# Two float16 parts in place of two float32r parts in the key and gate products of a channel mix

## The chip, the cores and the metric

The kernel runs on one core of one Trainium2 chip. The metric is device time of one execution in microseconds (us), the median of several runs. Three runs of the kernel before took 794.37, 796.18 and 797.66 us.

## The reference

Attention with a forgetting bias (8 batches, 8 heads, 576 positions, head width 64), and on its output `x` (8 x 576 rows of 512) a channel mix:

```python
xk = mu_k * x + (1.0 - mu_k) * x_prev      # x_prev: x one position earlier, zero first
xr = mu_r * x + (1.0 - mu_r) * x_prev
k = np.maximum(xk @ w_k, 0.0)              # 512 x 1024
v = k * k @ w_v                            # 1024 x 512
r = 1.0 / (1.0 + np.exp(-(xr @ w_r)))      # 512 x 512
return r * v
```

The weights arrive as float64 words and the result is wanted close to float32. A product therefore is made of three matmuls of operands in two parts, a high one and what is left: high·high, low·high, high·low.

## The kernel before

**Order.** Every piece of work is a task with an engine, an estimated duration, its buffers and a due time. `Plan.run` passes over all tasks forward and backward 30 times, keeps the order with the earliest modelled end, and emits each engine's instructions in it. The order is therefore fixed when the program is built, and any changed estimate moves instructions on all engines. `or_on` (through `or_dve`, `or_act`, `or_pool`) lets the planner put one task on a second engine. On PE, `pe(..., n, m, cycle)` charges `n * cycle` ns for n streamed columns.

**Attention.** 36 visits, each two heads of a batch. Batches 0 and 1 (12 visits, "plain") turn their weights on TensorE; batches 2 to 7 (24 visits) turn them by DMA and take values and weights as two float16 parts. There `greatest` finds on VectorE the largest amount of the values of each partition, `laid_out` spreads it over all rows by a small matmul, and three short VectorE and POOL instructions make the scale (`scales`). Queries and keys are split on POOL (`split_qk`), values too (`split_v`). Each visit stores its output to `x_d` in DRAM.

**Channel mix.** 18 chunks of 256 positions; `channel_mix` follows the attention by as much as `MARGIN` says. Of each chunk:
- `mix(0)` and `mix(1)`: for each pair of 128-row blocks, ACT multiplies x of one position by mu (L1432), VectorE adds the other position times 1 - mu (`mu1`, L1448), ACT copies the high part (L1470), VectorE subtracts for the low part (L1476). Parts are float32r.
- `hidden(fp)`, 4 times: 24 matmuls of 256 columns (L1504) into one bank, ACT Relu (L1516), VectorE product to the square (L1534), and two parts `kh`, `kl` (L1539, L1543).
- `gate(tt)`, twice: 12 matmuls of 512 columns (L1556), and tanh on ACT.
- `output(tt)`, twice: 24 matmuls of 512 columns with w_v (L1581), product with the gate (L1592), store.

So a chunk has 96 matmuls of 256 columns with w_k, 24 of 512 with w_r and 48 of 512 with w_v, and all 18 have 1728, 432 and 864.

**Weights.** `load_weight` joins two 32-bit words to a float32 (`whole`) on ACT, POOL and three VectorE steps (L654, L661, L668), copies the high part (L675) and subtracts for the low one (L680, on POOL or VectorE). All 8 blocks of w_k and 4 of w_r are loaded ahead of the visits, 8 of w_v in chunk 0.

When the TensorE queue has nothing ready in the first 40 us, the planner puts in small bfloat16 matmuls of no use (L434).

Of the kernel before, what the change touches and what calls it, by code (L numbers as in the profile page):

```python
# [11 lines left out]
F32 = mybir.dt.float32  # L12
# [42 lines left out]
class Plan:  # L55
# [24 lines left out]
    def __init__(self):  # L80
        self.tasks, self.slots, self.due = [], {}, 0.0
        self.columns, self.idle, self.busy_from = {}, None, None
        self.quarters = {}
        self.issues = {}
        self.others = {}
# [51 lines left out]
    def or_on(self, i, engine, ns, emit):  # L137
        self.others[i] = engine, ns, emit
# [198 lines left out]
def forgetting_attention_then_channel_mix(  # L337
# [20 lines left out]
    P = 128  # L358
# [30 lines left out]
    def pe(emit, reads, writes, n, m=P, cycle=1.05 / 2.4, k=P):  # L389
# [120 lines left out]
    mu = fixed(const.tile([P, 2, NC], F32, name="mu"))  # L510
    mu1 = fixed(const.tile([P, 2, NC], F32, name="mu1"))
# [46 lines left out]
    def early_sums():  # L558
# [15 lines left out]
        dve(lambda: nc.vector.memset(one.get(), 1.0), [], [one], n)  # L574
# [21 lines left out]
    def load_mu():  # L596
        for i, m in enumerate((moe_mu_k, moe_mu_r)):
            dma(lambda i=i, m=m: nc.sync.dma_start(mu.ap[:, i, :], m), [], [(mu, i)], 20)
        dve(
            lambda: nc.vector.tensor_scalar(  # L600
                out=mu1.ap, in0=mu.ap, scalar1=-1.0, scalar2=1.0, op0=ALU.mult, op1=ALU.add
            ),
            [(mu, 0), (mu, 1)], [mu1], 8,
        )

    def load_weight(name, c, o, w, due, x):
# [3 lines left out]
        tag = f"w_{name}_{c}_{o}"  # L610
        words = sbuf([P, 512, 2], tag, 1, I32)
        block = weight[name, c, o] = sbuf([P, 2, 512], tag, 1, F32R)
        hi, lo = (block, 0), (block, 1)
        plan.due = due - WAHEAD
# [9 lines left out]
        plan.due = due  # L624

        if name == "k":
            ps = bank(1, *(("xp", 1) if x % 3 == 2 else ("m", 2)))
        else:
            ps = bank(1, *(("xp", 1) if x % 2 == 0 else ("m", 2)))
        whole = sbuf([P, 512], (("xh1", "xl1") if name != "v" else ("x", "r"))[x % 2])  # L630

# [3 lines left out]
        def bits():  # L635
# [3 lines left out]
        last3 = sbuf([P, 512], "last3", 1, I32)  # L639
# [6 lines left out]
            [words], [last3], 512, 210, 1.0,  # L646
# [19 lines left out]
        )  # L666
        dve(
# [5 lines left out]
        )  # L673
        or_pool(
# [4 lines left out]
        def low(engine):  # L679
            engine.tensor_tensor(  # L680
                out=block.get()[:, 1], in0=whole.get(), in1=f32(block.get()[:, 0]), op=ALU.subtract
            )

        or_dve(
            pool(lambda: low(nc.gpsimd), [whole, hi], [lo], 512, 190, 2.0),
            lambda: low(nc.vector), 512, 200,
        )

# [10 lines left out]

    def greatest(n, vn):
        am = sbuf([P, 1], "am", 2, BF16)
        dve(
            lambda: nc.vector.tensor_reduce(
                out=am.get(), in_=vn.get()[:, 0:NQ].rearrange("p k h d -> p (k h d)"),
                axis=mybir.AxisListType.X, op=ALU.max, apply_absolute_value=True,
            ),
            [vn], [am], P * NQ,  # L710
# [3 lines left out]
    def laid_out(ps, a, am):  # L714
        pe(
            lambda: nc.tensor.matmul(
                ps.get()[:, a : a + P], am.get().broadcast_to([P, P]), ident16.ap,
                start=True, stop=True,
            ),
            [am, ident16], [ps], P, P, 1 / 2.4,  # L720
        )
        scales = sbuf([P, 3], "scales", 2)
# [5 lines left out]
        dve(  # L728
            lambda: nc.vector.tensor_reduce(
                out=own(0), in_=ps.get()[:, a : a + P], axis=mybir.AxisListType.X, op=ALU.max,  # L730
            ),
            [ps], [(scales, 0)], P,
        )
        dve(
            lambda: nc.vector.tensor_scalar(
                out=own(0), in0=own(0), scalar1=1.0e-28, scalar2=1.0 / HALF, op0=ALU.max, op1=ALU.mult,
            ),
            [], [(scales, 0)], 1,
        )
# [1092 lines left out]
```

## Time and profile before

| | |
|---|---|
| runs | 794.37, 796.18, 797.66 us |
| profiled execution | 794.96 us, of which the span from the first to the last instruction is 793.3 us |
| PE busy | 774.9 us, 98% |
| VectorE (DVE) busy | 625.0 us, 79% |
| ScalarE (ACT) busy | 607.8 us, 77% |
| GpSimd (POOL) busy | 414.1 us, 52% |
| granted TensorE clock | 1.00 of full speed in every stretch |

A matmul's duration in the trace is longer than the time by which it holds up the next one, since matmuls overlap. What one costs is read from a run of them back to back: the time of the run divided by their number. PEld, the loading of the stationary operand, overlaps the matmul before.

### The profile page before, as it was taken

What the parts mean: (1) busy time and instruction counts of PE and PEld (TensorE: products, weight loads), DVE (VectorE), ACT (ScalarE), POOL (GpSimd) and SP (SyncE); (2) the same over time, 40 slices, a digit from 0 to 9 for tenths busy, and PEclk for the clock granted to TensorE, in tenths of its full rate; (3) what the DMA queues carried; (4) which work ended last, traced back from release to release, by engine and by line L of the source; (5) the groups of instructions that cost most, each with busy time, mean ns of one, the idle gap of its engine ahead of it and who ended that gap; (6) DMA issues with size and microseconds to landing.
All of it is one profiled execution on the core that took longest, in us unless ns stands there. A gap on an engine that the chain in (4) does not pass through costs nothing. (4 is left out here: it accounts for less than half of the span.)

```text
span 793.3 us, 17133 instructions
## 1 busy us (share of the span) xinstructions
PE 774.9 (98%) x5369; PEld 654.2 (82%) x5369; DVE 625.0 (79%) x1886; ACT 607.8 (77%) x1847; POOL 414.1 (52%) x505
## 2 busy tenths in 40 slices
PE   9999899999999999999999999999999999999998
PEld 8878678868788887878887989787979788888996
DVE  7998978679888898779988898888889887444531
ACT  5998988779878887879888887878888887444420
POOL 5896966664756746666656565467466610000000
PEclk9999999999999999999999999999999999999999
DMA  7967364379999888977989898897978756111000
GB/s 223 287 222 236 100 178 121 86 174 191 188 189 191 175 205 171 206 134 174 214 177 189 191 188 200 157 180 179 213 140 193 144 117 118 50 54 41 14 27 26
DMA packets 220155, 124.15 MB, mean 157 GB/s; under 512 B 180192, under 2 KB 193504, under 8 KB 220064
## 3 DMA queue, kind: packets, MB, share of 16 engines
q1 hardware_dynamic: 220064, 123.06, 69.2%
q8 instruction: 42, 0.69, 0.4%
q14 instruction: 49, 0.40, 0.2%
HBM read 61.21 MB, written 19.33 MB: 102 GB/s over the span
## 5 line engine op out<-in xcount | busy, mean ns | idle before, releaser
L1504 PE MATMUL m<-xh,w_k 128*128 128x256 f32 x976 | 193.4, 286 | 2.9 <-DVE kl L1543 2.2
L1581 PE MATMUL m<-w_v,kh 128*128 128x512 f32 x528 | 177.3, 400 | 0.0
L1504 PEld LDWEIGHTS m<-xh,w_k 128*128 128x128 f32 x976 | 156.6, 189 | 8.5 <-DVE kl L1543 5.1
L1504 PE MATMUL m<-xl,w_k 128*128 128x256 f32 x488 | 138.6, 284 | 0.0
L1581 PEld LDWEIGHTS m<-w_v,kh 128*128 128x128 f32 x528 | 99.0, 189 | 19.8
L1581 PE MATMUL m<-w_v,kl 128*128 128x512 f32 x264 | 105.5, 399 | 0.2 <-DVE kl L1543 0.2
L1432 ACT ACTIVATE xp<-x,mu 128x256 f32<-128x256 f32 (+3 forms) x179 | 76.0, 425 | 27.3 <-DMA x<-x_d 15.3
L839 POOL TENSOR_TENSOR KH<-raw,KH 64x576 fp32r<-64x576 f32 x64 | 91.2, 1425 | 5.6 <-ACT KH L828 1.4
L1504 PEld LDWEIGHTS m<-xl,w_k 128*128 128x128 f32 x488 | 92.2, 189 | 1.0
L1556 PE MATMUL m<-w_r,xh 128*128 128x512 f32 x264 | 91.3, 400 | 0.5 <-DVE kl L1543 0.5
L1448 DVE SCALAR_TENSOR_TENSOR xp<-x,mu,xp 128x256 f32<-128x256 f32 (+3 forms) x184 | 76.5, 416 | 18.6 <-ACT xp L1432 15.5
L863 POOL TENSOR_TENSOR QL<-raw,G 64x576 fp32r<-64x576 f32 (+1 forms) x64 | 85.3, 1333 | 3.8 <-ACT G L852 1.0
L1019 ACT ACTIVATE s<-s,nm 128x64 f32<-128x64 f32 (+2 forms) x144 | 61.3, 425 | 17.4 <-DVE nm L1004 15.9
L859 POOL CAST G<-raw 128x576 fp32r<-128x576 f32 x48 | 32.0, 666 | 78.7 <-issue 56.1
L1050 DVE SCALAR_TENSOR_TENSOR W<-s,rinv,W 128x64 f16<-128x64 f32 (+2 forms) x144 | 64.2, 456 | 11.0 <-ACT W L1044 9.2
L1044 ACT ACTIVATE W<-s,rinv 128x64 f16<-128x64 f32 (+2 forms) x144 | 63.5, 456 | 6.2 <-DVE rinv L1035 5.1
L1050 DVE SCALAR_TENSOR_TENSOR W<-t,rinv,W 128x320 f16<-128x320 f32 (+1 forms) x96 | 61.4, 645 | 6.5 <-ACT W L1044 5.7
L1019 ACT ACTIVATE t<-t,nm 128x320 f32<-128x320 f32 (+1 forms) x96 | 55.3, 576 | 8.4 <-DVE nm L1004 5.3
L1476 DVE TENSOR_TENSOR xl<-xp,xh 128x512 fp32r<-128x512 f32 x72 | 49.4, 687 | 12.4 <-ACT xh L1470 12.0
L1004 DVE CUSTOM_DVE_ANT_0 t<-t,lower 128x512 f32<-128x512 f32 (+1 forms) x96 | 57.2, 601 | 2.4 <-PE t L992 2.0
L1556 PEld LDWEIGHTS m<-w_r,xh 128*128 128x128 f32 x264 | 49.5, 188 | 11.2 <-DVE kl L1543 1.4
L1044 ACT ACTIVATE W<-t,rinv 128x320 f16<-128x320 f32 (+1 forms) x96 | 57.5, 609 | 1.7 <-DVE rinv L1035 1.0
(206 smaller groups left out, 1990.6 us busy)
## 6 DMA issues: line engine op xcount, KB each, us to landing
raw<-in_q SPq DMA_DIRECT2D x112, 144.0 KB
raw<-in_k SPq DMA_DIRECT2D x32, 288.0 KB
vn<-in_v SPq DMA_DIRECT2D x24, 384.0 KB
out<-g SPq DMA_DIRECT2D x36, 256.0 KB
x_d<-xT SPq DMA_DIRECT2D x28, 288.5 KB
x<-x_d SPq DMA_DIRECT2D x11, 514.0 KB
w_k<-in_moe_w_k SPq DMA_DIRECT2D x8, 512.0 KB
w_v<-in_moe_w_v SPq DMA_DIRECT2D x8, 512.0 KB
```

The source lines that it names most:

```text
L839: lambda own=own, other=other, K=K: nc.gpsimd.tensor_tensor(out=K.get()[other], in0=k.get()[own], in1=f32(K.get()[own]), op=ALU.subtract),
L863: lambda x=x, QQ=QQ, QL=QL: nc.gpsimd.tensor_tensor(out=QL.get()[0:64, 0:nq], in0=x.get()[0:64], in1=f32(QQ.get()[0:64]), op=ALU.subtract,),
L1004: lambda: nc.vector.tensor_tensor_reduce(out=ps.get()[:, :n], in0=ps.get()[:, :n], in1=mask(), scale=-SCALE, scalar=3.0e38, op0=ALU.add, o ...
L1019: lambda: nc.scalar.activation(ps.get()[:, :n], ps.get()[:, :n], AF.Exp, bias=nm.get()[:, i + o : i + o + 1], scale=-1.0, accum_out=sums.g ...
L1044: lambda: nc.scalar.activation(part(0), ps.get()[:, :n], AF.Copy, scale=rinv.get()[:, i : i + 1]),
L1050: lambda: nc.vector.scalar_tensor_tensor(out=part(1), in0=ps.get()[:, :n], scalar=rinv.get()[:, i : i + 1], in1=part(0), op0=ALU.mult, op1 ...
L1432: lambda z=z: nc.scalar.activation(to(*z), source(1, *z), AF.Copy, scale=mu.ap[:, which, c + z[0] : c + z[0] + 1]),
L1448: lambda z=z: nc.vector.scalar_tensor_tensor(out=to(*z), in0=source(0, *z), scalar=mu1.ap[:, which, c + z[0] : c + z[0] + 1], in1=to(*z), ...
L1476: lambda: nc.vector.tensor_tensor(out=lo.get()[:, cc], in0=src(), in1=f32(hi.get()[:, cc]), op=ALU.subtract),
L1504: lambda u=u, f=f, c=c, n=n, w=w, x=x: nc.tensor.matmul(ps.get()[:, u * CT : (u + 1) * CT], weight["k", c, f // 4].get()[:, w, f % 4 * P : ...
L1556: lambda c=c, n=n, x=x, w=w: nc.tensor.matmul(ps.get(), x.get()[:, c, ts], weight["r", c, 0].get()[:, w], start=c == 0 and n == 0, stop=c ...
L1581: lambda f=f, n=n, x=x, w=w: nc.tensor.matmul(ps.get(), x.get()[:, f, ts], weight["v", f, 0].get()[:, w], start=f == 0 and n == 0, stop=f ...
```

## The change

Products with w_k and w_r take two float16 parts. Float16 has a short range of exponents, so both operands are scaled by powers of two:
- `load_rows` finds the largest amount of each weight row (128 x 512, both halves of w_k), cuts it to its exponent (`steps`), and multiplies the row by its inverse times 2^14 on POOL before the two parts are made.
- `scale_mu` multiplies mu and 1 - mu (now one tile `mus`) by `steps`, and finds the largest of them over all rows by a small matmul (`most`).
- `greatest` now runs for the plain visits too; the largest value of each batch is kept in `tops`. `scale_chunk` makes of `tops` and `most` a power of two for the batches of a chunk and the scaled `shares`, in five or six short VectorE instructions. It runs again only when the set of batches differs from that of the chunk before: 15 times for each of the two products.
- Relu, square and tanh take the scale out again, by constants or by a scalar of each partition.

The number of matmuls stays. The planner's numbers change as well: columns of float16 matmuls are charged less, of float32r more, `MARGIN` is 5000, a few tasks may go to another engine than before (`free` holds that to batches 0 and 1 and chunks 0 to 2), some memsets and the low part of the weights are now always on POOL, and w_r is loaded in chunk 0 after the second `hidden` and not ahead of the visits.

```diff
-    def pe(emit, reads, writes, n, m=P, cycle=1.05 / 2.4, k=P):
+    def pe(emit, reads, writes, n, m=P, cycle=1.07 / 2.4, k=P):
...
     def or_on(self, i, engine, ns, emit):
-        self.others[i] = engine, ns, emit
+        if self.free:
+            self.others[i] = engine, ns, emit
...
+    def all_rows(ps, am, a=0):
+        pe(
+            lambda: nc.tensor.matmul(
+                ps.get()[:, a : a + P], am.get().broadcast_to([P, P]), ident16.ap,
+                start=True, stop=True,
...
+    def scale_mu(which):
+        both = mus.ap[:, which]
+        am = sbuf([P, 1], "am", 2, BF16)
+        ps = bank(1, "xp", 1)
...
+                out=both, in0=both, in1=steps.ap[:, which].unsqueeze(1).broadcast_to([P, 2, NC]),
...
+            [(steps, (which, c)) for c in range(NC)], [(mus, which)], 8,
...
+        all_rows(ps, am)
...
+                out=most.ap[:, which : which + 1], in_=ps.get()[:, 0:P],
...
+    def load_rows(which, c, due, step):
...
+            block = weight[name, c, o] = sbuf([P, 2, 512], f"w_{name}_{c}_{o}", 1, F16)
...
+            join(words[o], ps, whole, (found, o, lambda o=o: found.get()[:, o : o + 1]))
...
+                own().bitcast(I32), own().bitcast(I32), EXPONENT, op=ALU.bitwise_and
...
+            lambda: nc.vector.reciprocal(found.get()[:, 2:3], own()), [key], [(found, 2)], 1,
...
+                lambda whole=whole: nc.gpsimd.tensor_scalar(
+                    out=whole.get(), in0=whole.get(), scalar1=found.get()[:, 2:3], scalar2=2.0**14,
...
+            parts_of(block, whole)
+        if c == NC - 1:
+            scale_mu(which)
...
+    def scale_chunk(which, groups):
...
+                out=own(0), in_=tops.ap[:, a:e].rearrange("p a b -> p (a b)"),
...
+                out=own(1), in0=own(0), scalar1=most.ap[:, which : which + 1], scalar2=1.0e-30,
...
+                own(1).bitcast(I32), own(1).bitcast(I32), EXPONENT, op=ALU.bitwise_and
...
+        dve(lambda: nc.vector.reciprocal(own(2), own(1)), [], [scaled], 2)
...
+                out=shares.get(), in0=mus.ap[:, which], scalar1=own(2), scalar2=0.25,
...
         def mix(which):
-            hi = sbuf([P, NC, CT], f"xh{which}", 1, F32R)
-            lo = sbuf([P, NC, CT], f"xl{which}", 1, F32R)
+            hi = sbuf([P, NC, CT], f"xh{which}", 1, F16)
+            lo = sbuf([P, NC, CT], f"xl{which}", 1, F16)
             st[which] = (hi, lo)
+            st["scales", which] = scales(which)
...
-                            [(weight["k", c, f // 4], w), (x, c)], [ps], CT,
+                            [(weight["k", c, f // 4], w), (x, c)], [ps], CT, P, 1 / 2.4,
...
-                    out=sq(), in0=sq(), scalar=0.0, in1=r.get(), op0=ALU.max, op1=ALU.mult,
+                    out=sq(), in0=sq(), scalar=scaled.get()[:, 3:4], in1=r.get(),
+                    op0=ALU.mult, op1=ALU.mult,
...
-                lambda: nc.scalar.activation(g.get(), ps.get(), AF.Tanh, scale=0.5),
+                lambda: nc.scalar.activation(
+                    g.get(), ps.get(), AF.Tanh, scale=scaled.get()[:, 1:2]
...
+        groups = sorted({0 if ch == 0 else 1 + b for b, _, _, _ in segs} | ({0} if segs[0][0] == 0 else set()))
...
-    MARGIN = 25000.0
+    MARGIN = 5000.0
```

**How instructions move.** On PE, in a gate of chunk 16 (behind the last attention), the order before has one row for each matmul, `xh` and `xl` being the two parts of x, `w_r` the weights, `po` the bank:

```order
L1556 MATMUL po_87<-w_r_00_631,xh_925 128x512
L1556 MATMUL po_87<-w_r_00_631,xl_944 128x512
L1556 MATMUL po_87<-w_r_00_631,xh_925 128x512
L1556 MATMUL po_87<-w_r_00_661,xh_925 128x512
L1556 MATMUL po_87<-w_r_00_661,xl_944 128x512
L1556 MATMUL po_87<-w_r_00_661,xh_925 128x512
```

With the change the same gate reads:

```order
L1773 LDWEIGHTS xh_1227
L1773 MATMUL po_89<-w_r_00_1021,xh_1227 128x512
L1773 LDWEIGHTS xl_1236
L1773 MATMUL po_89<-w_r_00_1021,xl_1236 128x512
L1773 LDWEIGHTS xh_1227
L1773 MATMUL po_89<-w_r_00_1021,xh_1227 128x512
L1773 LDWEIGHTS xh_1227
L1773 MATMUL po_89<-w_r_00_1089,xh_1227 128x512
```

The matmuls stand in the same sequence, each with its load of the stationary operand as an instruction of its own, as the float16 products of the attention had already.

On VectorE, ahead of the first chunk's `mix(0)`, the order before has the joining of w_r's words (L654 to L668) into `xp`, `m` and the whole words `xl`, `xh`, and then, behind an output of the first visits (L1375), the first product of x and mu:

```order
L654 TENSOR_SCALAR xp_317<-xp_317 128x512
L668 SCALAR_TENSOR_TENSOR xl_91<-w_r_00_487,m_197 128x512
L661 SCALAR_TENSOR_TENSOR xp_317<-xp_317,last_195 128x512
...
L668 SCALAR_TENSOR_TENSOR xh_328<-w_r_00_531,xp_317 128x512
...
L1375 TENSOR_TENSOR w_v_00_231<-po_87,w_v_00_231 128x320
L1448 SCALAR_TENSOR_TENSOR xp_317<-w_v_00_225,mu_73,xp_317 128x256
```

With the change the first product of x stands behind `most`, the scale of the chunk (`scaled`) and the `shares`, with masked scores of the attention (L1081, `nm`) between them:

```order
L656 TENSOR_REDUCE most<-xp_331 128x1
L1563 TENSOR_REDUCE scaled_759<-tops 128x1
...
L1571 TENSOR_SCALAR scaled_724<-scaled_724,most 128x1
L1081 ISA W_165,nm_166<-s_142,lower 128x448
...
L1578 TENSOR_SCALAR scaled_724<-scaled_724 128x1
...
L1583 RECIPROCAL scaled_724<-scaled_724 128x1
...
L1585 TENSOR_SCALAR shares_785<-mus,scaled_724 128x8
L1653 TENSOR_SCALAR xp_331<-w_v_00_270,shares_785 128x256
...
L1661 SCALAR_TENSOR_TENSOR xp_331<-w_v_00_263,shares_785,xp_331 128x256
```

The joining of w_r has moved behind this place, and the first L1661 now comes after the whole chain of scales.

On VectorE in a later chunk, the two chains of short instructions (`scaled_724` for w_k, `scaled_759` for w_r) run into one another and stand between attention instructions:

```order
L1571 TENSOR_SCALAR scaled_724<-scaled_724,most 128x1
L1563 TENSOR_REDUCE scaled_759<-tops 128x1
L1578 TENSOR_SCALAR scaled_724<-scaled_724 128x1
L1571 TENSOR_SCALAR scaled_759<-scaled_759,most 128x1
L1583 RECIPROCAL scaled_724<-scaled_724 128x1
L1081 ISA W_165,nm_166<-s_136,lower 128x448
...
L1585 TENSOR_SCALAR shares_785<-mus,scaled_724 128x8
L1578 TENSOR_SCALAR scaled_759<-scaled_759 128x1
L1127 RECIPROCAL inverses_236<-inverses_236 128x5
```

There was nothing of the kind before; L1127 is the inverse of a sum of weights, which stood in the old order too.

## Rows read from the trace of the kernel before

**Rows 1.** Page: span; busy us (share of the span) and instructions by engine.

```profile
span 793.3 us, 17133 instructions
...
PE 774.9 (98%) x5369; PEld 654.2 (82%) x5369; DVE 625.0 (79%) x1886; ACT 607.8 (77%) x1847; POOL 414.1 (52%) x505
```

**Rows 2.** Windows of all engines: us, then busy us (instructions) of each engine, clock.

```profile
0.00:180.00 180.00, 173.38 (x1338) 144.11 (x1339) 150.54 (x454) 149.90 (x457) 130.89 (x182) 1.00 0.62 180
180.00:680.00 500.00, 492.04 (x3391) 414.15 (x3391) 427.43 (x1353) 416.50 (x1311) 283.21 (x324) 1.00 0.86 176
680.00:793.30 113.30, 109.46 (x643) 95.96 (x642) 47.05 (x82) 41.43 (x81) 0.00 (x0) 1.00 0.10 32
```

**Rows 3.** Windows of line L1504 (products with w_k) alone.

```profile
0.00:180.00 180.00, 32.13 (x192) 26.56 (x192) 1.00 0.62 180
180.00:680.00 500.00, 158.85 (x1183) 149.94 (x1184) 1.00 0.86 176
680.00:793.30 113.30, 43.03 (x355) 42.52 (x354) 1.00 0.10 32
```

**Rows 4.** Windows of line L1556 (products with w_r) alone.

```profile
0.00:180.00 180.00, 13.71 (x48) 8.54 (x48) 1.00 0.62 180
180.00:680.00 500.00, 76.22 (x288) 52.65 (x288) 1.00 0.86 176
680.00:793.30 113.30, 23.19 (x96) 17.75 (x96) 1.00 0.10 32
```

**Rows 5.** Chain that ended last, by time: start us, us, what.

```profile
721.87 11.22 PE m L1581 x48
733.10 5.70 PE t L1504 x48
...
744.51 2.79 PE po L1556 x12
```

**Rows 6.** Timeline of PE, 16-bit matmuls: start us, us from first start to last end.

```profile
26.74 0.74 PE L434 MATMUL po<-ident 128*128 128x192 bf16 x7
...
37.50 0.25 PE L434 MATMUL po<-ident 128*128 128x192 bf16 x1
```

**Rows 7.** Timeline of PE, a float16 block of the attention.

```profile
306.62 2.20 PE L1180 MATMUL po<-T,V 128*64 128x512 f16 x28
308.65 0.23 PE L1180 MATMUL s<-T,V 128*64 128x64 f16 x4
```

**Rows 8.** Lines of DVE by form: busy us, mean ns | idle before, releaser.

```profile
L1534 DVE SCALAR_TENSOR_TENSOR m<-m,r 128x512 f32<-128x512 f32 x61 | 42.9, 703 | 11.5 <-ACT r L1516 10.9
...
L1050 DVE SCALAR_TENSOR_TENSOR W<-t,rinv,W 128x512 f16<-128x512 f32 x48 | 35.8, 746 | 3.2 <-ACT W L1044 3.0
...
L706 DVE TENSOR_REDUCE am<-vn 128x1 bf16<-128x640 f32 x24 | 19.5, 812 | 2.5 <-DMA vn<-in_v 2.4
...
L654 DVE TENSOR_SCALAR m<-m 128x512 f32<-128x512 f32 x12 | 8.3, 689 | 1.8 <-ACT m L649 1.8
...
L740 DVE RECIPROCAL scales<-scales 128x1 f32<-128x1 f32 x24 | 3.8, 158 | 0.4
```

**Rows 9.** Lines of POOL by form.

```profile
L641 POOL TENSOR_SCALAR last<-w_k 128x512 int32<-128x512 uint8 x8 | 5.5, 684 | 8.6 <-DVE m L661 3.9 <-DMA w_k<-in_moe_w_k 3.1 <-DVE nm L934 1.3
...
L680 POOL TENSOR_TENSOR w_v<-x,w_v 128x512 fp32r<-128x512 f32 x3 | 3.9, 1286 | 0.9 <-ACT w_v L675 0.8
```

**Rows 10.** Timeline of DVE before the first chunk.

```profile
36.91 0.16 DVE L980 RECIPROCAL inverses<-inverses 128x3 f32<-128x3 f32 x1
37.00 0.65 DVE L668 SCALAR_TENSOR_TENSOR xl<-w_k,m 128x512 int32<-128x512 int32 x1
...
44.23 1.00 DVE L1448 SCALAR_TENSOR_TENSOR xp<-w_v,mu,xp 128x256 f32<-128x256 f32 x2
```

**Rows 11.** Waits of PEld: us in total, times, longest us.

```profile
PEld s L992 <- DVE W L1050: 10.1, 19, 1.5
PEld m L1504 <- DVE kl L1543: 5.1, 11, 1.3
```

More of the change, by code (lines that the diff above doesn't have):

```diff
@@ L573, in early_sums @@
         )
[L574 removed]
+        pool(lambda: nc.gpsimd.memset(one.get(), 1.0), [], [one], n, 160)
         pool(
@@ L623, in load_weight, with join @@
         )
[L624 to L630, printed above, removed]
+        return words
+    def join(words, ps, whole, top=None):
         def word(i):
@@ L666, in load_weight @@
         )
+        if top:
+            to, key, ap = top
+            dve(
+                lambda: nc.vector.tensor_reduce(
+                    out=ap(), in_=ps.get(), axis=mybir.AxisListType.X, op=ALU.max
+                ),
+                [ps], [(to, key)], 512,
+            )
         dve(
@@ L673, in load_weight, with parts_of @@
         )
+    def parts_of(block, whole):
+        hi, lo = (block, 0), (block, 1)
         or_pool(
@@ L1073, in last_and_first @@
             if am:
-                values = laid_out(side, P, am)
+                values = laid_out(side, P, am, top)
             least(side, 64, lambda: corners_mask.ap, c)
@@ L1412, in mixed, with share @@
         def mixed(which, c, xm):
+            shares = st["scales", which][0]
+            def share(i, c):
+                return shares.get()[:, i, c : c + 1]
             todo = [(y, i, n, o) for y in range(2) for i, (_, _, n, o) in enumerate(segs)]
@@ L1450, in mixed @@
                         in0=source(0, *z),
-                        scalar=mu1.ap[:, which, c + z[0] : c + z[0] + 1],
+                        scalar=share(1, c + z[0]),
                         in1=to(*z),
@@ L1455, in mixed @@
                     ),
-                    parts(*z[:2]) + [mu1] + [(xm, ("a", *u)) for u in todo],
-                    [(xm, ("d", *z))], z[2], extra=250 if z is not todo[-1] else 130,
+                    parts(*z[:2]) + [shares] + [(xm, ("a", *u)) for u in todo],
+                    [(xm, ("d", *z))], z[2], extra=130,
                 )
@@ L1600, in output, with scales @@
             )
+        groups = sorted({0 if ch == 0 else 1 + b for b, _, _, _ in segs} | ({0} if segs[0][0] == 0 else set()))
+        def scales(which):
+            if chunk_scales.get(which, [None])[0] != groups:
+                chunk_scales[which] = groups, scale_chunk(which, groups)
+            return chunk_scales[which][1]
         at(-XLEAD)
```

417 lines of the change are left out of this document (286 added, 131 removed).

## The prediction

> **What bounds the kernel now.** I read the page's busy shares first, then the windows by stage, then the chain that ended last, and then runs of single lines. The page has PE at 98% [rows 1], but matmuls overlap in the trace, so that share alone says little. The windows say more: PE is busy 492 of 500 us between 180 and 680 us and 109.5 of 113.3 us behind that, always at the full granted clock (1.00, that is 2.4 GHz), while VectorE falls from 427 us in 500 to 47 in 113 [rows 2]. Behind 680 us the attention is over and TensorE alone sets the time: the chain that ended last is there nothing but channel-mix matmuls back to back, and their true price can be read [rows 5]: 11.22 us for 48 of 512 columns with w_v is 233.8 ns each, 5.70 us for 48 of 256 columns with w_k is 118.8 ns, 2.79 us for 12 with w_r is 232.5 ns. All three cost about 0.46 ns a column. Between 180 and 680 us TensorE is nearly as full, but VectorE is busy 85% and ScalarE 83% of it [rows 2], so a change that gives TensorE less and VectorE more has to be weighed there. Before 180 us PE is idle 6.6 us, VectorE 29.5 us, POOL 49 us [rows 2].
>
> **The gain: columns of float16.** The count of matmuls stays; their columns get cheaper if float16 streams faster than float32r. Two groups show 16-bit operands. A float16 block of an attention visit (28 matmuls in 14 pairs of two heads that run side by side) goes from 306.62 to 308.65 us [rows 7]; by `todo` in `sum_values` the pairs have 4 x 512, 2 x 448, 2 x 320, 384, 2 x 192, 256 and 2 x 64 columns, 4736 in all, so 2.03 us is 0.429 ns a column. The useless bfloat16 matmuls, which load 128 x 128 for each 192 columns, take (0.74 - 0.25) / 6 = 81.7 ns each, 0.425 ns a column [rows 6]; so a 16-bit load of 128 columns is hidden even behind 192, and will be behind 256. Between the two I take 0.427: 109.3 ns for 256 columns and 218.6 for 512. The new products save 118.8 - 109.3 = 9.5 ns and 232.5 - 218.6 = 13.9 ns each. By stretch [rows 3, 4]:
> - to 180 us: 192 and 48 matmuls, 1.8 + 0.7 = 2.5 us
> - 180 to 680 us: 1183 and 288, 11.2 + 4.0 = 15.2 us
> - behind 680 us: 355 and 96, 3.4 + 1.3 = 4.7 us
>
> Together 22.4 us. With 0.429 for all it would be 21 us, with 0.425 it would be 23.5.
>
> The Trainium skill (TensorE: Matmul & The Clock Gate, Back-to-back issue gap) gives a lone warm matmul N/2.4 + 2.5 ns, that is 109.2 ns for 256 columns and 215.8 for 512; by it the sum would be 9.6 x 1728 + 16.7 x 432 = 23.8 us. The rows of w_v, float32r, are 18 ns above that rule, so it does not hold for float32r here, and what speaks for it in 16 bits is rows 6.
>
> **What comes on top, before 180 us.** VectorE gets 12 reductions of 128 x 512 in PSUM, no row of which exists; the nearest, L654 over the same operand, takes 689 ns [rows 8], so 8.3 us. It gets 12 reductions of the plain visits' values at 812 ns or less (L706) [rows 8], at most 9.7 us, and some 77 instructions on one to eight columns (28 for the weight rows, 7 for mu, 9 for the batches' maxima, 33 for the scales of the first three chunks). One of these takes 158 ns alone (L740) [rows 8], and holds the queue for 90 ns where the next needs nothing of it (36.91 to 37.00 us) [rows 10]: 6.9 to 12.2 us. So VectorE has at most 30 us more, against 29.5 us of idle time [rows 2], and five low parts of weights and five memsets leave it for POOL. POOL gets 12 multiplications of 512 at about 684 ns (L641) and five low parts at 1286 ns (L680) [rows 9], 8.2 + 6.4 us, and the memsets, against 49 us idle [rows 2]. If all of VectorE's surplus came into the path it would be some 22 us (30 less about 8 for what leaves); if the idle time takes it, nothing. I take 2 us, near the covered end, since chunk 0 to 2 are few and TensorE has the plain visits beside them.
>
> The new wait: `mix(0)` of chunk 0 now needs the scale of all w_k rows. Behind it stand ACT's copies and all of the first `hidden`, for which TensorE waits. Before, the last word of w_k was joined at 37.00 us and the first product with mu began at 44.23 us [rows 10]; the 7.2 us between held w_r's joining, which the change moves behind. The new chain there is some 13 short instructions, 13 x 158 ns = 2.1 us, and one small matmul. It fits, so I cost it at nothing; without that cover it would be 2.5 us.
>
> **What comes on top, 180 to 680 us.** Twelve sets of scales with eleven short instructions, 132 x 90 to 158 ns = 12 to 21 us on VectorE, and the square's scalar of each partition instead of a constant: L1050 with such a scalar takes 746 ns, L1534 703 [rows 8], so 43 ns more for some 48 of them, 2 us. VectorE's 427 us become 441 to 450 us in a stretch that should be 485 long, 91 to 93%. The order puts the two chains of a chunk into one another and between attention instructions, and they need only the batch's maxima, known long before `x`. So they fill idle time; what they cost is a little more waiting of TensorE, which waits for VectorE 10.1 us and 5.1 us at its weight loads over the span [rows 11]. From nothing to the whole 23 us, I take 1 us. Gate and mix on ACT change only in a scalar and a type of output; no cost. Behind 680 us VectorE has 66 us idle and nothing new is on the path.
>
> **Sum.** The profiled execution took 794.96 us, 1.2 under the median of the runs. 794.96 - 22.4 + 2 + 1 = 775.6 us. Predicted: 775.5.
>
> **Rivals.**
> *More than the columns.* The planner gets truer charges and a smaller margin, so chunks come earlier and fill TensorE's idle time. There is 6.6 + 8 us of idle before 680 us [rows 2] and 15 us of waits at the loads [rows 11]; if half of the first and a few us of the second went, 767 us or less. Against it: the margin orders work that TensorE has anyway.
> *Half lost.* VectorE and ScalarE at 85% and 83% [rows 2] are coupled with TensorE; with 91% and more on VectorE, TensorE's waits grow by half of what the middle gains: 775.6 + 7.6 = 783 us, up to 790 if nearly all of it goes. For it: the waits at the loads are already for VectorE [rows 11]. Against it: 72 us of idle VectorE time in the middle.
> *Slower: VectorE becomes the bound of the middle.* If the 72 us of idle there are not free but steps in which VectorE waits for ScalarE's half of the softmax, nothing more can be put in. Then the middle's gain of 15.2 us is gone and the new short instructions count in full: 794.96 - 4.7 + 18 = 808 us. It decides from the point where an added VectorE instruction in the middle delays the next visit's scores. Against it stands TensorE's 492 us of 500.
> *The change does not do what it says: float16 is no faster.* If a 256-column product stays at 118.8 ns, what is left is the added work, 795 to 800 us. For it: the visible floor could be the drain or the load and not the type. The Trainium skill (FP8 and Floating Point Precision, TensorE Precision Notes) has float16 raised to the format to which reduced float32 is cut, at one pass each; by that rule alone the sum would be nothing. Against it: 0.425 and 0.429 ns a column in 16 bits, 0.46 in float32r, in the same program at the same clock [rows 5 to 7].
>
> **How the numbers follow.** The forecast (770 to 781) 0.58, more than the columns 0.12, half lost 0.15, VectorE the bound 0.09, float16 no faster 0.06. A measurement of this kernel can tell about 0.5%, 4 us, from no change: 792.2 to 800.2. Faster is the first three but for the end of the third: 0.58 + 0.12 + 0.13 = 0.83; same 0.06 + 0.02 = 0.08; slower 0.09. The range goes from 766 us, into the first rival, to 787 us, into the half-lost case; what is left out is 0.06 below and the upper third of the half-lost case with the last two above.
>
> **What would show it.** Right: 48 products with w_k back to back at the end take 5.2 to 5.3 us, 12 with w_r 2.6 us, w_v's 48 stay at 11.2; PE stays at 97% or more of the middle; VectorE is about 91% busy there; the first product with w_k starts no later than 50 us. Wrong: products with w_k still at 118 ns; long waits of PEld for VectorE in the middle; a VectorE at 95% with PE below 95%; a first chunk that starts many us later, with PE idle in front of it.

## The result and the profile after

The changed kernel takes 804.9 us (median of 4 runs, 804.2 to 805.3) against 796.0 us before: a ratio of 1.0105, 95% interval 1.0080 to 1.0131. It is 1.0% slower; 775.5 was forecast. The profiled execution took 804.19 us, 28.6 more than the sum of 775.6.

The page and the same three windows as in [rows 1, 2]:

```profile
span 802.4 us, 17403 instructions
## 1 busy us (share of the span) xinstructions
PE 763.4 (95%) x5383; PEld 570.0 (71%) x5383; DVE 658.4 (82%) x2096; ACT 615.1 (77%) x1862; POOL 427.6 (53%) x526
```

```profile
0.00:180.00 180.00, 167.40 (x1311) 126.96 (x1311) 154.39 (x510) 145.95 (x445) 136.42 (x194) 0.99 0.58 173
180.00:680.00 500.00, 477.40 (x3308) 352.35 (x3308) 442.68 (x1458) 414.44 (x1300) 291.22 (x333) 1.00 0.81 173
680.00:802.40 122.40, 118.57 (x769) 90.68 (x767) 61.32 (x129) 54.70 (x118) 0.00 (x0) 1.00 0.21 53
```

TensorE's busy time fell by 11.5 us, not 22.4, and its idle time rose from 18.4 to 39.0 us, by 20.6. The difference of the two, 9.1, is that of the spans.

The products themselves cost what the forecast said. The chain at the end (start, us, what) answers to [rows 5]:

```profile
734.02 11.10 PE m L1800 x48
745.12 5.25 PE t L1720 x48
...
774.53 5.24 PE s L1720 x48
...
782.39 5.18 PE m L1773 x24
```

48 products with w_k take 5.24 us (109.2 ns each, 118.8 before), 24 with w_r 5.18 us (215.8, 232.5 before), and w_v, still float32r, takes 231 (233.8 before). Equal cuts hide where the time went, because stages moved. I cut at the attention's float16 blocks instead (the matmuls that [rows 7] time): *early* is before the first of them, *middle* from the first to the last, *tail* behind it. Their first block stands at 184.0 us before and 192.1 after:

```profile
L1180 PE MATMUL po<-T,V x28: 193/312/403, 184.0 to 186.0; 128*64 128x512 f16 x8, 128*64 128x448 f16 x4, 128*64 128x320 f16 x4, 128*64 128x192 f16 x4
```

```profile
L1334 PE MATMUL po<-T,V x23: 246/352/403, 192.1 to 194.0; 128*64 128x512 f16 x8, 128*64 128x448 f16 x4, 128*64 128x320 f16 x4, 128*64 128x192 f16 x4
```

Windows with these cuts, before and then after:

```profile
0.00:184.00 184.00, 177.38 (x1360) 147.38 (x1361) 153.90 (x463) 153.46 (x468) 134.52 (x185) 1.00 0.62 181
184.00:679.00 495.00, 487.04 (x3364) 409.92 (x3363) 423.37 (x1341) 412.22 (x1297) 279.58 (x320) 1.00 0.86 176
679.00:793.30 114.30, 110.46 (x658) 96.92 (x654) 47.74 (x83) 42.14 (x82) 0.00 (x0) 1.00 0.10 32
```

```profile
0.00:192.10 192.10, 178.93 (x1361) 135.66 (x1361) 165.31 (x546) 155.09 (x475) 144.82 (x202) 0.99 0.59 171
192.10:701.80 509.70, 487.57 (x3447) 360.88 (x3446) 447.91 (x1466) 420.63 (x1311) 282.82 (x325) 1.00 0.80 172
701.80:802.40 100.60, 96.87 (x586) 73.44 (x582) 45.18 (x85) 39.37 (x77) 0.00 (x0) 1.00 0.11 36
```

The tail is 13.7 us shorter: 72 products with w_k moved from it into the middle (8.6 us at 118.8 ns), and what stayed got cheaper. The early part is 8.1 us longer, the middle 14.7. TensorE's idle time is 13.2 us early (6.6 before) and 22.1 in the middle (8.0 before).

What the idle time ends with shows at the weight loads (us in total, times, longest), against 10.1 us in [rows 11]:

```profile
PEld s L1139 <- DVE W L1204: 21.3, 36, 2.2
PEld L1720 <- issue: 16.2, 50, 1.1
PEld s L1139 <- ACT xT L1362: 7.3, 13, 1.0
PEld t L1385 <- ACT T L1413: 7.2, 12, 2.0
```

The scores of the next pass wait for a PSUM tile that VectorE's half of the softmax frees: 11 us more. What the loads of w_k wait for, 16.2 us, the trace does not name ("issue").

VectorE's lines, new or changed (by form: busy us, mean ns | idle before), against what was assumed from [rows 8]:

```profile
L1748 DVE SCALAR_TENSOR_TENSOR m<-m,scaled,r 128x512 f32<-128x512 f32 x61 | 46.0, 753 | 4.7 <-ACT r L1733 4.2
...
L1585 DVE TENSOR_SCALAR shares<-mus,scaled 128x8 f32<-128x8 f32 x30 | 16.4, 548 | 0.4
...
L852 DVE TENSOR_REDUCE amounts<-V 128x1 bf16<-128x640 f32 x8 | 6.4, 806 | 0.0
L1571 DVE TENSOR_SCALAR scaled<-scaled,most 128x1 f32<-128x1 f32 x30 | 6.0, 207 | 5.7 <-ACT g L1785 5.1
...
L716 DVE TENSOR_REDUCE found<-m 128x1 f32<-128x512 f32 x8 | 5.4, 674 | 0.0
```

A reduction takes 674 ns (689 assumed), the square with a scalar of each partition 753 (746). The short instructions were sized too low: L1585, eight columns times a scalar of each partition, takes 548 ns against at most 158, and L1571 207. By the trace the short ones take 18.6 us of VectorE to 180 us, against 6.9 to 12.2, and all the new ones 34.4, against 30 at most.

Early, VectorE is full. Windows of 15 us, before, then after, and then a_nowork, the changed kernel without its scaling (Experiments):

```profile
60.00:75.00 15.00, 15.00 (x112) 13.67 (x112) 12.27 (x31) 12.72 (x29) 9.03 (x12) 1.00 0.77 238
```

```profile
60.00:75.00 15.00, 13.10 (x111) 10.20 (x111) 15.00 (x45) 11.75 (x31) 14.06 (x16) 0.89 0.58 184
```

```profile
60.00:75.00 15.00, 14.00 (x107) 9.48 (x105) 14.74 (x37) 13.55 (x33) 13.86 (x17) 1.00 0.72 226
```

Before, TensorE has no gap there and VectorE 2.7 us of idle time; after, it is VectorE that has none. That alone does not convict the scaling: without it VectorE has 0.3 us of idle time there, and in after the joining of words, those of w_r among them since the change, takes 6.2 us of the window, as much as the new instructions (6.1). VectorE's timeline inside that window (start, us) shows what stands in its queue: an early maximum (L852), pieces of a weight's maximum (L790, L796, L802, L716) and the joining of words (L700), between the attention's steps:

```profile
60.07 0.81 DVE L852 TENSOR_REDUCE amounts<-V 128x1 bf16<-128x640 f32 x1
60.80 0.45 DVE L1081 CUSTOM_DVE_ANT_0 W<-s,lower 128x288 f32<-128x288 f32 x1
...
61.24 0.69 DVE L700 TENSOR_SCALAR xp<-xp 128x512 f32<-128x512 f32 x1
...
63.09 0.15 DVE L802 RECIPROCAL found<-steps 128x1 f32<-128x1 f32 x1
```

And TensorE's, with a gap of 1.54 us that ended with ScalarE, and behind it products with w_k at half the rate:

```profile
65.23 0.44 PE L1385 MATMUL t<-ident,W 128*128 128x128 f32 x2 [1.54 <-ACT xT L1530]
...
68.21 0.64 PE L1720 MATMUL m<-xh,w_k 128*128 128x256 f16 x2
68.64 0.42 PE L1720 MATMUL m<-xl,w_k 128*128 128x256 f16 x1
68.85 0.63 PE L1720 MATMUL m<-xh,w_k 128*128 128x256 f16 x2
```

From 68.21 to 68.64 and to 68.85 us it is 0.21 us a product, not 0.109.

### The profile page after: what moved, and what is told of

Its sections match the earlier page's. It is cut to its first block, busy times and chain, and to the rows that moved or that the text cites. A ratio compares the mean times of both kernels' runs of the same rounds, so it can differ in the third digit from the quotient of the medians.

```text
span 802.4 us, 17403 instructions
## 1 busy us (share of the span) xinstructions
PE 763.4 (95%) x5383; PEld 570.0 (71%) x5383; DVE 658.4 (82%) x2096; ACT 615.1 (77%) x1862; POOL 427.6 (53%) x526
## 4 chain that ended last, share of the span: by engine, by line
PE 36%; DVE 28%; ACT 21%; issue 7%; DMA 4%; POOL 1%; SPq 1%; ACTq 0%; DVEq 0%; POOLq 0%
PE m L1800 7%; PE m L1773 5%; DVE W L1204 5%; PE m L1720 4%; ACT W L1192 4%; DVE xp L1661 4%; ACT t L1166 3%; ACT xp L1648 3%; ACT s L1166 3%; PE po L1334 3%; DVE t L1151 3%; DVE s L1151 2%; PE t L1800 2%; PE s L1139 2%; PE t L1720 2%
## 5 line engine op out<-in xcount | busy, mean ns | idle before, releaser
L1720 PEld LDWEIGHTS <-w_k 128*128 128x128 f16 x1728 | 163.5, 98 | 38.2 <-issue 16.2
L1720 PE MATMUL m<-xh,w_k 128*128 128x256 f16 x976 | 175.9, 274 | 6.8 <-DVE kl L1759 4.2
L1720 PE MATMUL m<-xl,w_k 128*128 128x256 f16 x488 | 133.6, 274 | 0.3 <-DVE xl L1690 0.3
L1661 DVE SCALAR_TENSOR_TENSOR xp<-x,shares,xp 128x256 f32<-128x256 f32 (+3 forms) x184 | 76.7, 417 | 23.2 <-ACT xp L1648 19.8
L1648 ACT ACTIVATE xp<-x,shares 128x256 f32<-128x256 f32 (+3 forms) x180 | 76.4, 425 | 21.1 <-DVE xl L1690 12.3
L1773 PE MATMUL m<-w_r,xh 128*128 128x512 f16 x264 | 84.7, 381 | 1.2 <-DVE kl L1759 1.0
L1139 PE MATMUL s<-KH,G 128*128 128x64 f32 (+2 forms) x192 | 56.7, 312 | 12.6 <-DVE W L1204 9.1
L1204 DVE SCALAR_TENSOR_TENSOR W<-t,rinv,W 128x512 f16<-128x512 f32 (+1 forms) x96 | 61.3, 644 | 7.4 <-ACT W L1192 7.0
L1166 ACT ACTIVATE t<-t,nm 128x512 f32<-128x512 f32 (+1 forms) x96 | 55.4, 577 | 8.8 <-DVE nm L1151 4.5
L1192 ACT ACTIVATE W<-t,rinv 128x512 f16<-128x512 f32 (+1 forms) x96 | 57.1, 607 | 3.0 <-DVE rinv L1182 2.0
```

The costliest lines, as they stand in the source:

```text
L1139: lambda x=x, G=G, K=K, r=r: nc.tensor.matmul(ps.get()[:m, :n], G.get()[:r, q : q + m], K.get()[:r, k0 : k0 + n], start=x == 0, stop=x == 1,),
L1166: lambda: nc.scalar.activation(ps.get()[:, :n], ps.get()[:, :n], AF.Exp, bias=nm.get()[:, i + o : i + o + 1], scale=-1.0, accum_out=sums.g ...
L1192: lambda: nc.scalar.activation(part(0), ps.get()[:, :n], AF.Copy, scale=rinv.get()[:, i : i + 1]),
L1204: lambda: nc.vector.scalar_tensor_tensor(out=part(1), in0=ps.get()[:, :n], scalar=rinv.get()[:, i : i + 1], in1=part(0), op0=ALU.mult, op1 ...
L1648: lambda z=z: nc.scalar.activation(to(*z), source(1, *z), AF.Copy, scale=share(0, c + z[0])),
L1661: lambda z=z: nc.vector.scalar_tensor_tensor(out=to(*z), in0=source(0, *z), scalar=share(1, c + z[0]), in1=to(*z), op0=ALU.mult, op1=ALU.a ...
```

## Experiments

Labels with b are the kernel before with an edit, labels with a the changed kernel with an edit. "No scaling" leaves out the powers of two and all that finds them; the two float16 parts stay. All are timed against the kernel before on the same chip (its medians: 796.2 to 797.5). The stages are of the profiled execution.

```
label                 us     ratio [95%]              early  middle  tail
before                796.0                           184.0  495.0  114.2
after                 804.9  1.0105 [1.0080, 1.0131]  192.1  509.7  100.6
a_m25                 837.0  1.0506 [1.0439, 1.0572]  208.3  514.6  110.3
b_m5                  788.2  0.9893 [0.9843, 0.9944]  180.5  499.0  105.4
a_charges             795.9  0.9991 [0.9972, 1.0011]  190.8  505.0   99.4
b_f16                 789.6  0.9912 [0.9889, 0.9934]  192.9  486.6  109.7
b_f16_m5              780.1  0.9774 [0.9757, 0.9792]  178.2  501.8  100.3
a_nowork              789.9  0.9903 [0.9885, 0.9920]  179.5  508.4  100.8
a_oldplan             792.9  0.9937 [0.9921, 0.9953]  192.1  499.2   99.8
a_nowork_oldplan      776.2  0.9720 [0.9694, 0.9745]  175.1  501.5   99.9
a_noweights           804.2  1.0103 [1.0084, 1.0122]  193.9  507.8  100.6
a_nosteady            793.1  0.9962 [0.9948, 0.9976]  183.1  509.0  100.8
a_cycle               800.1  1.0049 [1.0033, 1.0066]  187.2  508.4  100.5
a_nowork_oldplan_m1   773.5  0.9722 [0.9702, 0.9742]  170.7  500.7   99.5
a_noamax              805.3  1.0103 [1.0077, 1.0129]  185.2  514.5  100.6
a_oldplan_m1          808.2  1.0142 [1.0124, 1.0160]  198.8  508.6   99.5
a_cycle106            810.0  1.0173 [1.0152, 1.0193]  191.5  515.6  100.8
b_f16_m1              778.3  0.9781 [0.9746, 0.9816]  177.5  498.7   99.3
a_nosteady_oldplan    778.7  0.9778 [0.9752, 0.9803]  180.9  499.5   99.1
a_nowork_cycle106     783.4  0.9843 [0.9822, 0.9863]  176.6  502.6  100.8
```

**MARGIN, the charges of the x mix, float16 alone.** The first theory was that the planner's numbers in the diff (a smaller MARGIN, smaller charges for the x mix) spoil the order.

```diff
-    MARGIN = 5000.0
+    MARGIN = 25000.0
```

> The changed kernel with MARGIN 25000 again. Margin theory: 778 to 788 us. Added-work or charge theory: 800 to 806 us, no better than the changed kernel's 804.9.

> The kernel before with MARGIN 5000 in place of 25000 alone. Margin theory (channel work due 20 us earlier stands in front of the attention's softmax steps): 803 to 815 us, the last attention block ends 8 us or more later than 679 us. If the margin is not it (the added VectorE work or the charges are): 794 to 798 us.

```diff
-                        parts(*z[:2]) + [shares], [(xm, ("a", *z))], z[2], 190,
+                        parts(*z[:2]) + [shares], [(xm, ("a", *z))], z[2], 290,
...
-                    [(xm, ("d", *z))], z[2], extra=130,
+                    [(xm, ("d", *z))], z[2], extra=250 if z is not todo[-1] else 130,
```

> The changed kernel with the old charges of the x mixing (ACT 290 and VectorE 250 ns over the columns, in place of 190 and 130). Charge theory (the planner takes the mixing for 120 ns shorter than it is, so that queues stand in a wrong order): 780 to 792 us. Margin or added-work theory: 802 to 807 us.

> The kernel before with float16 parts for the products with w_k and w_r and their lower charge, and nothing else of the change; it leaves out all scaling by powers of two. If the added VectorE work, the margin or the charges made the changed kernel slow, TensorE's 22 us come through here: 772 to 779 us. If less TensorE work turns into waits for VectorE and ScalarE anyway (the softmax sets the middle), 787 to 796 us, with PE under 97% of the middle.

MARGIN as the cost is refuted: the old value makes the changed kernel 32 us slower, and the new one makes the kernel before 8.4 us faster. No theory had expected 837. Part of it is TensorE's granted clock, 0.94 early:

```profile
0.00:208.30 208.30, 188.18 (x1372) 142.31 (x1372) 168.89 (x550) 158.58 (x480) 142.72 (x200) 0.94 0.54 160
```

That is at most some 12 us lost (208.3 us times 0.06, an estimate), against some 2 in after, with 0.99. The old charges give back 9.0 us and VectorE's waits for ScalarE in the x mix shorten (us in total, times, longest; after, then a_charges):

```profile
DVE xp L1661 <- ACT xp L1648: 20.7, 28, 4.2
```

```profile
DVE xp L1661 <- ACT xp L1648: 15.7, 20, 1.7
```

The charge of before, 256/0.96 + 250 = 517 ns by the planner's formula, is nearer to the two products with mu that took 1.00 us together [rows 10] than the new one of 397. Float16 alone gives 7.0 us, not 22.4: the upper of its two expectations.

**Scaling work and planner numbers apart.** Four kernels, each with float16 and MARGIN 5000. "Old numbers" takes back the charges, and with them the choices of engine and the memsets of before. The edits' core:

```diff
--- no scaling
-            join(words[o], ps, whole, (found, o, lambda o=o: found.get()[:, o : o + 1]))
+            join(words[o], ps, whole)
...
-            st["scales", which] = scales(which)
-            scaled = st["scales", 0][1]
+            scaled = fixed_scales
...
-        greatest(vn, -(-KN[tiles[-1]] // P), amounts[-1], hp)
--- old numbers
-    def pe(emit, reads, writes, n, m=P, cycle=1.07 / 2.4, k=P):
+    def pe(emit, reads, writes, n, m=P, cycle=1.05 / 2.4, k=P):
...
-            [vn, (V, 0)], [(V, 1)], n, 190, 2.0,
+            [vn, (V, 0)], [(V, 1)], n, 210, 2.21,
```

> The kernel before with float16 parts (products charged at one cycle per column) and MARGIN 5000; no scaling, all other charges of the planner as before. If the gains of the two runs that made one of these edits each (7.0 and 8.4 us) add, about 781 us. If the float16 products give what their duration says once the order suits them (22 us) and the margin adds its own, 766 to 774. If both edits only move the same wait, 786 to 790.

> The changed kernel without the scaling: no row maxima of the weights, no multiplication of them on GpSimd, no maxima over the batches, no scales of x; constants stand in their place. All of the planner's numbers as in the changed kernel. Theory 1, the added work is the cost (VectorE and GpSimd get it on the path to a chunk's weights and to its x): 775 to 785. Theory 2, the planner's new numbers are the cost: 792 to 802, no more than some 5 us under the changed kernel.

> The changed kernel with its scaling and all its float16 products, but with the planner's numbers of before (cycle 1.05, the charges of the x mix and of GpSimd's subtractions, halves and sums of values on ScalarE alone, memsets on VectorE, low parts on GpSimd or VectorE); MARGIN 5000 and the place of the w_r loads stay as in the changed kernel. Theory 1, the added work is the cost: 792 to 805. Theory 2, the numbers are the cost: 775 to 786. The old charges of the x mix alone gave 795.9.

> Both edits: no scaling work and the planner's numbers of before. It is then close to the kernel before with float16 and MARGIN 5000, but for the loads of w_r, which start in chunk 0. Both theories: within 5 us of that run. If it is over 8 us slower, the early loads of w_r are a cost of their own. If both causes add, it lies below the other two by the amount of each.

b_f16_m5 came where the two single gains add (about 781 expected, 780.1). By these four both theories hold, each for about half. Without the scaling it is 15.0 us less with the new numbers and 16.7 with the old; the old numbers give 12.0 us with the scaling and 13.7 without. The table says where: the scaling costs early (192.1 against 179.5, and 192.1 against 175.1), the numbers in the middle (10.5 and 6.9 us).

**Which part of the scaling, and how much is luck of the order.**

> The changed kernel without the scaling of the weights alone: no row maxima, no powers of two from them, no multiplication on GpSimd; a constant 2^14 takes their place in the x mix. The scales of x by batch stay. All the scaling together cost 15 us on these numbers of the planner, nearly all of it before the first pass of the steady attention (192.1 against 179.5 us). Theory, the chain to chunk 0's first weight is what costs (it waits for the maxima of both halves and for GpSimd): 790 to 794. Rival, the maxima of the early values and the batch scales on VectorE cost: 800 to 804.

> The changed kernel without the scales of x: no maxima of the early values, no powers of two by batch, no shares; constants stand in their place. The scaling of the weights stays. Theory, the weights' chain costs: 800 to 804. Rival, the early maxima and the batch scales cost: 790 to 794. If both share the 15 us by their VectorE time (about 11 us of 180 early for the x scales, 9 for the weights): about 797 for each of the two runs.

> The changed kernel with one of the planner's numbers of before, the charge of 1.05 cycles for a column of the other matmuls instead of 1.07; no work is added or removed. A test of how far the time moves when the order is merely dealt again: if the gains of the other runs are such luck, this one lies 5 us or more from the changed kernel too, on either side. If they are causes, it stays within 3 us: 802 to 808.

> The fastest so far (no scaling work, the planner's numbers of before, 776.2) with MARGIN 1000 instead of 5000. Going from 25000 to 5000 gained 8 us in the kernel before. If that was a reserve given back, the rest of it is worth up to 2 us: 773 to 777. If it is only another deal of the order: 770 to 784.

The theory that the weights' chain is the main cost falls. Without it the first product with w_k starts at 44.0 us instead of 52.0, and the end gains 0.7 us. Two more pairs, in which the scales of x are out already, give the weights 3.2 us (a_nosteady to a_nowork) and 2.5 (a_nosteady_oldplan, below, to a_nowork_oldplan), too little to tell from a deal of the order. The scales of x, which I had as the rival, are worth 11.8. But a_cycle, in which no work changes, moved by 4.8 us: a new deal of the order (another order from the planner, for the same work) is worth about as much as some of these differences. So the next runs repeat the question under other deals.

> The changed kernel without the maxima of the early values alone (12 reductions of about 0.72 us on VectorE, and what gathers them for each batch): a constant stands in their place in the batch scales, which are still computed for each chunk. Without all the scaling of x it ran in 793.1, 11.8 us less than the changed kernel. If the 12 reductions (8.6 us of VectorE before 190 us) are what holds the early part up: 794 to 798. If the scales of each chunk (eight runs of 0.56 us early, and the waits of the x mix for them) are: 801 to 804.

> All of the changed kernel's work, with the planner's numbers of before and MARGIN 1000 instead of 5000: the version that keeps the scaling. With MARGIN 5000 it took 792.9; without the scaling the same step of MARGIN gained 2.7 us. Expected 788 to 793. If MARGIN is luck of the order: 786 to 798.

> The changed kernel with 1.06 in place of 1.07 for a column of the other matmuls; 1.05 gave 800.1. If the number itself is what gained (the planner's PE now runs too slow in its plan), this lies between: 801 to 804. If the order is only dealt again with every number: anywhere from 798 to 808, outside of 800 to 805 as likely as in it.

> The kernel before with float16 parts and MARGIN 1000; with 5000 it took 780.1. If MARGIN is a reserve of which the rest is worth 2 to 3 us: 776 to 780. If luck of the order: 774 to 788. It also shows whether the changed kernel's early w_r loads are worth anything: with the same MARGIN and without the scaling that kernel took 773.5.

> The changed kernel without the scales of x (constants stand in their place) and with the planner's numbers of before; the weights are still scaled. By stages, as the runs so far have them: the first pass of the steady attention starts near 183 us without the scales of x (against 187 to 199 with all the scaling), the middle takes near 501 us with the old numbers (against 505 to 516 with the new), the tail 100: 783 to 788. If the scales of x are not what holds the early part up and 183.1 was luck of the order, its start lies at 190 or later and the time at 792 or more.

> The changed kernel without any scaling work, with the planner's new numbers but 1.06 for 1.07: a second deal of the order for a_nowork (789.9, middle 508.4). If the new numbers are a cause, the middle stays at 505 us or more and the time at 784 or more. If the middle of a_nowork was luck, it falls to the 499 to 502 of the kernels with the old numbers, and the time to 775 to 782.

With 1.06, between 1.05 and 1.07, the time is 810.0, above both: that number is a deal and no cause. MARGIN 1000 instead of 5000 gives 2.7 and 1.8 us without the scaling and takes 15.3 with it, a miss by 15 us. Hence single differences under some 10 us between two of these kernels prove nothing, the 9.0 us of a_charges among them, and I go by groups. Six kernels with all of the scaling at MARGIN 5000 or 1000 take 792.9 to 810.0 (mean 802.0), six with float16 and without any 773.5 to 789.9 (mean 780.2): they do not overlap, and neither do their early parts, 187.2 to 198.8 against 170.7 to 179.5 (means 192.1 and 176.3). More of the first six have the new numbers, four against two, but with like numbers the times stay apart as well: 795.9 to 810.0 against 783.4 and 789.9 with the new, 792.9 and 808.2 against 773.5 to 780.1 with the old. The scales of x were taken out twice, 11.8 and 14.2 us, both times with an early part of 181 to 183 us (the second run came out 4 us below its expectation). A third pair is on record: with the weights' scaling out already, taking the scales of x out as well gives 14.3 us (a_noweights to a_nowork, early part 193.9 to 179.5). Windows of the early part and the middle, first of a_oldplan, then of a_nosteady_oldplan, which differ by the scales of x alone:

```profile
0.00:192.10 192.10, 180.13 (x1380) 137.72 (x1380) 179.61 (x561) 153.68 (x477) 139.27 (x196) 0.99 0.58 171
192.10:691.30 499.20, 484.54 (x3452) 360.69 (x3451) 446.86 (x1466) 420.47 (x1308) 280.07 (x322) 1.00 0.84 176
```

```profile
0.00:180.90 180.90, 171.58 (x1317) 132.70 (x1317) 160.76 (x493) 155.13 (x479) 136.98 (x194) 0.98 0.60 180
180.90:680.50 499.60, 487.99 (x3469) 363.02 (x3467) 431.35 (x1354) 418.79 (x1307) 281.61 (x323) 1.00 0.86 176
```

VectorE has 18.9 us less to do early, and the stage is 11.2 us shorter. In the middle it has 15.5 us less to do, and nothing is gained: there the added work was covered. a_noamax starts its middle at 185.2 us, which speaks for the early maxima, and loses it again in the middle; with one deal of it, which half of the scales costs stays open. The new numbers of the planner cost 12.0, 14.4 and 13.7 us in the three pairs at MARGIN 5000, but a_nowork_cycle106 came out 6.5 us below a_nowork with its middle at 502.6, where the theory wanted 505 or more, and a_oldplan_m1 has a long middle with the old numbers. Their cost is likely and its size is not settled. The rest of the change, with the later loads of w_r, is no cost: at MARGIN 5000 and 1000 the kernel with it is 3.9 and 4.8 us below b_f16_m5 and b_f16_m1.

The fastest version with all the scaling is a_oldplan, 792.9 (0.5 to 0.8% below the kernel before, no more than one deal), the fastest without it a_nowork_oldplan_m1, 773.5.

## Why the prediction was wrong, step by step

*The gain per product* was right: 109.2 and 215.8 ns measured, 109.3 and 218.6 forecast. The rival of no faster float16 is dead.

*Where the gain counts* failed. The sum took every nanosecond of the 15.2 us in the middle as time, because TensorE is busy 492 of 500 us there [rows 2]. b_m5 and b_f16_m5 differ by float16, by the lower charge of its columns, and so by the deal of the order. Their first two stages:

```profile
0.00:180.50 180.50, 176.20 (x1371) 147.15 (x1372) 153.12 (x461) 152.54 (x471) 132.82 (x184) 1.00 0.62 182
180.50:679.50 499.00, 493.81 (x3431) 419.58 (x3430) 427.39 (x1346) 414.23 (x1302) 282.42 (x323) 1.00 0.83 175
```

```profile
0.00:178.20 178.20, 171.20 (x1324) 132.88 (x1324) 152.05 (x455) 149.77 (x464) 127.62 (x178) 0.98 0.63 183
178.20:680.00 501.80, 490.29 (x3464) 363.21 (x3464) 428.55 (x1354) 416.72 (x1311) 283.70 (x325) 1.00 0.84 175
```

Early it gains 2.3 us, in the tail 5.1 (4.7 forecast), and in the middle it loses 2.8, while TensorE's idle time there rises from 5.2 to 11.5 us. But these stages do not hold the same work. 18 products with w_v (4.2 us at 231 ns) that stand early in b_m5 stand in the middle in b_f16_m5. Windows of the middle, products with w_v alone (busy us of PE and PEld, clock):

```profile
180.50:679.50 499.00, 149.62 (x576) 105.88 (x576) 1.00 0.83 175
```

```profile
178.20:680.00 501.80, 157.87 (x594) 108.51 (x594) 1.00 0.84 175
```

So the two stages have to be read together. The last attention block ends at 679.5 us in b_m5 and at 680.0 in b_f16_m5, and the same pair at the old MARGIN, before and b_f16, has 679.0 and 679.5 (early and middle of the table). Of the 17.7 us that the forecast had before the tail nothing arrives in either pair; the tail gives 5.1 and 4.5. (The medians differ by 8.1 and 7.0 us, so by them some 3 may arrive.) Part of what is missing is the granted clock, which early is 0.98 in both float16 kernels and 1.00 in the two others: at most some 4 us of each early part (178.2 and 192.9 us times 0.02, an estimate). b_f16's early part:

```profile
0.00:192.90 192.90, 180.89 (x1388) 141.81 (x1388) 155.38 (x466) 155.76 (x479) 136.26 (x188) 0.98 0.61 176
```

The busy share had misled me. A product with w_k shows as 274 ns in the page of after,

```profile
L1720 PE MATMUL m<-xh,w_k 128*128 128x256 f16 x976 | 175.9, 274 | 6.8 <-DVE kl L1759 4.2
```

and in the tail one follows the last at 109, so a stall shorter than the rest leaves no idle time in a window. The Trainium skill (Perfetto Trace Analysis, Identifying the Most-Contended Engine) warns that matmul busy time is no measure of how near the bound a kernel is, since matmuls are pipelined; the 493.81 and 490.29 us here, for work that differs by some 10 us at the prices of the forecast (15.8 in the cheaper products, less some 6 that moved in), agree. All kernels with the old numbers and MARGIN 5000 or 1000 have a middle of 498.7 to 501.8 us, with or without the scaling, but for a_oldplan_m1; only b_m5 among them is without float16. That some chain of VectorE, ScalarE and TensorE in the attention sets it is my reading; which wait it is was not isolated. Against it stand before and b_f16, whose middles are shorter, 495.0 and 486.6 us, with fewer products with w_k in them (1176 and 1131, against 1243 in b_m5 and 1248 in b_f16_m5).

*What comes on top, before 180 us*, 2 us in the sum, failed as well: 12.6 and 17.0 us in the two pairs, 15.8 between the groups' means. The short instructions were sized too low (18.6 us against 12.2 at most). And the idle time that was to take the new work was counted over 180 us, 29.5 us. Two windows of before, beside the one from 60 to 75 us above:

```profile
15.00:45.00 30.00, 29.12 (x253) 23.73 (x253) 29.21 (x89) 28.06 (x99) 23.61 (x28) 1.00 0.85 261
...
105.00:180.00 75.00, 73.30 (x558) 60.19 (x557) 57.42 (x199) 58.84 (x191) 48.98 (x61) 1.00 0.51 135
```

VectorE's idle time is 0.8 us from 15 to 45 us and 2.7 from 60 to 75, where by the trace of after 12.6 and 6.1 us of the new instructions fall; 17.6 of the 29.5 us lie behind 105. The bound named there, 22 us if all of it came into the path, was near the truth, and the choice of the covered end the mistake. *Chunk 0's wait* at no cost: its first product came 4.7 us later (52.0 against 47.3), but in a_noweights, where it comes 8.0 us earlier, the end gains only 0.7, which speaks against this delay as the cost.

*What comes on top, the middle*, 1 us: right for the scaling, as both pairs without the scales of x show (509.7 and 509.0; 499.2 and 499.5).

*The planner's numbers* had no term of their own. They hold the largest gain, MARGIN's, 8.4 and 9.5 us in the two pairs of b kernels (part of what the rival "more than the columns" named), and likely a cost of about 12. Step by step through runs that each change one group of things, each step one deal of the order: before to b_m5 -8.4, float16 -8.1, the rest of the changed code without scaling -3.9 (a_nowork_oldplan), scaling of the weights +2.5, scales of x +14.2, the new numbers +12.0; together +8.3, for 8.9 measured.

Of the signs named beforehand, the products' prices came as for "right"; the longer waits of the weight loads for VectorE and the later first chunk came as for "wrong", and TensorE came at 95% of the middle window, but beside a VectorE of 89%, not 95%.

*The slower rival* gave 808 us and came nearest in time and half in mechanism: VectorE did run out of idle time and the gain before the tail did vanish, but VectorE's place was the early part, and the gain vanishes without any added work on VectorE (b_f16, b_f16_m5).

## What to carry to other kernels

Before a gain on one engine counts as time, make that engine cheaper in one stage by experiment, and count the work in the stage, since a new order moves it; a busy share of 98% for pipelined matmuls is no proof that it is the bound. Weigh added work against the idle time of the 15 us in which it falls, not of the stage. And where a planner deals the order, one kernel is one draw: change a number that means nothing, see how far the time moves, and only believe effects that are larger or that repeat under other deals.

## What the runs showed of the hardware

TensorE's granted clock fell in the middle of a kernel, where it was 1.00 throughout in the profiled execution of before (other executions of before have a mean of 0.994 to 0.998). In windows of 5 us of after:

```profile
60.00:65.00 5.00, 3.69 (x37) 2.65 (x36) 5.00 (x15) 4.95 (x13) 4.70 (x6) 1.00 0.75 241
65.00:70.00 5.00, 4.42 (x23) 3.52 (x24) 5.00 (x13) 3.57 (x10) 4.63 (x5) 0.66 0.54 178
```

After 1.3 us of idle time in the first it is granted 0.66 in the second, the mean of stretches at 2.4 and 1.2 GHz, and the products there run at 0.21 us. (5 us at 0.66 is at most 1.7 us lost, an estimate.) The cost of a wait on TensorE can then be more than the wait. The Trainium skill (TensorE: Matmul & The Clock Gate, HAM oscillation) describes a clock that falls back after gaps inside a running kernel; the row of 65 to 70 us agrees with it. Idle time does not always bring it. A longer gap, of 1.78 us, ends at 80.40 us, and the clock stays at 1.00 until 90 us:

```profile
80.40 0.41 PE L1385 MATMUL t<-ident,W 128*64 128x128 f32 x2 [1.78 <-ACT T L1413]
```

How much this moves a kernel of one fixed order shows in ten executions of a_cycle: the four with a mean granted clock of 1.000 took 797.5 to 798.3 us, the two with 0.991 took 801.2 and 803.1.

A short VectorE instruction does not have one price: L1585, 128x8 in every one of its 30 executions, took from 205 to 1641 ns (median 375), L783, 128x1, from 146 to 1293. What makes them long was not looked into.
